# Batch 0's q slots 2 and 3 as one load, permuted on GpSimd; its kv masked by one product; tile 1 turned sooner

## The chip, the core and the metric

The kernel runs on one core of a Trainium2 chip. The metric is the device time of one execution in microseconds (us); five runs of the kernel before gave a median of 294.08.

The core's engines run side by side, each in its own program order: PE (TensorE, matrix multiplications), DVE (VectorE), ACT (ScalarE), POOL (GpSimd) and SP (SyncE, which here only issues transfers). They wait for one another through semaphores. Loads from DRAM are issued here by POOL, since they convert float32 to bfloat16 on the way; stores and transposing transfers are issued by SP. PE's results land in PSUM, where ACT and DVE read them.

## The reference

A linear attention is followed by a two-layer network with a residual:

```python
batch, n_heads, seq, head_dim = (8, 8, 576, 64)     # d_model 512, hidden 2048
kv  = np.einsum('bhsd,bhse->bhde', k, v)            # 64x64 for each head
out = np.einsum('bhsd,bhde->bhse', q, kv)
rms = np.sqrt(np.mean(out * out, axis=-1, keepdims=True) + 1e-06)
x   = out / rms * g_norm                            # then heads side by side: 512 wide
mu, var = mean and variance of x over 512
xn  = (x - mu) / np.sqrt(var + 1e-06) * g_ln
y   = x + np.maximum(xn @ w_ch1, 0.0) @ w_ch2
```

## The kernel before, in words

**Tiles.** The 8 x 576 rows are 36 tiles of 128 rows. A batch gives four tiles, t = 0 to 3, of every fourth row (row 4p + t lies on partition p), and the fifths, the last 64 rows of two neighbouring batches, share a tile. Each tile goes through a chain. `t_out` (PE, L475) multiplies the transposed q (qT) by kv. ACT squares it (`t_sq`, L488), DVE reduces the squares (L497) and multiplies by g_norm (xg, L492), ACT takes the root (L501), DVE the reciprocal (inv, L506) and the product x (L523), then the mean (L535, L539) and xc = (x - mean) * g_ln (L549). xc is transposed: for the first twelve tiles by PE (`t_turn_pe`, L556) and copied to xT by ACT (L563), for later ones by a transposing transfer. The factor 1/std is applied at the end, in `y_out` (L647).

**Main work.** The first layer of tiles 0 to 7 runs tile by tile (`m1_fine`, L606, 16 matmuls of 128 columns for each of four chunks of w1), for later tiles in blocks of four (`m1_block`, L621). ACT evicts with the relu (L613, L628). The second layer is `m2` (L640), four matmuls of 512 columns for each chunk of w2. A chunk, c = 0 to 3, is 512 of the 2048 hidden columns. w1 and w2 are loaded once, chunk by chunk (`load_w`, L343 and L345).

**kv.** `kv_mm` (L452) multiplies k and v of two heads at once, a 128x128 product whose two diagonal blocks of 64x64 are wanted. `kv_out` copies these two blocks into kv_pack, whose other blocks hold zeros. For batch 0 this is done in three parts (heads 0 to 3, 4 and 5, 6 and 7): the upper block by ACT (L465) and the lower by DVE (L467), into a kv_pack that ACT has zeroed (L378).

**q.** For batch 0 each of the slots t = 0 to 3 is a load of its own, straight into the layout that the transposes read (`load_slot`, L262: 64 floats at a time from DRAM). For batch 1 one load brings all four slots (`load_q`, L248) into a buffer qb, and ACT permutes it slot by slot into that layout (`q_permute`, L391). PE transposes a slot (`q_turn_pe`, L411), and ACT or DVE copies the result to qT.

**What sets the order.** The program order on each engine is not the order of the Python code. Every operation is recorded as a step with an engine, an estimated cost, a key (its due place) and the steps that it needs (`add`, L97). `run_plan` (L107) then runs a small simulation: among the steps that can start at the earliest time, the one with the smallest key goes first. On POOL the recorded order is kept as it is, and a step of the main work (`main=True`) keeps its place among the next eight of its kind. At most eight transfers of POOL are under way at a time: an issue waits until the one eight before it has landed. Before the first main step, PE's gaps in the plan are filled with matmuls on a blank tile (`idle_mm`, L961), in numbers taken from the plan.

So a changed load, cost or key can move instructions on all engines. Around the change, POOL's program is: k, v and slot 0 of batch 0 in parts, the identity, slot 1 (L262), then chunks of w1 and slots 2 and 3 in turn, six memsets (L380 to L385), and `load_w_kv1` (L351): w2 chunk 0, k and v of batch 1, w2 chunk 1, q of batch 1 and the rest of w2.

Tile 0 is worked in two halves of heads (`HALVED`, L53). Tiles 0 and 1 have xc and its turn in two halves (`HALF_TURN`, L55). `behind_first` (L667) ties the turn of q's slot 2 behind the turn of tile 0.

Of the kernel before, what the change touches and what calls it, by code (L numbers as in the profile page):

```python
# [14 lines left out]
def kernel(  # L15
# [11 lines left out]
    nc = tc.nc  # L27
# [177 lines left out]
    nc.vector.memset(eps_attn, EPS_ATTN)  # L205
    eps_ln = consts.tile([128, 1], f32, name="eps_ln")
    nc.vector.memset(eps_ln, EPS_LN)
    warm = consts.tile([128, 1], f32, name="warm")
    nc.scalar.activation(warm, eps_ln, func=AF.Sqrt)

# [97 lines left out]
    load = {}  # L308
# [30 lines left out]
    def load_w(c, which):  # L339
        dst, src = ((w1, w1_src), (w2, w2_src))[which - 1]  # L340
        def fn():
            if which == 1:
                nc.gpsimd.dma_start(dst[c], src[:, :, c * 512:(c + 1) * 512])  # L343
            else:
                nc.gpsimd.dma_start(dst[c], src[:, c * 4:(c + 1) * 4, :])  # L345
        pool_load(("w", which, c), (fn, 512 * 512 * 4))
# [2 lines left out]
        make_identity(nc, identity)  # L349

    def load_w_kv1():  # L351
        load_w(0, 2)
        pool_load(("k", 1), load_kv(kb, k, 1), rate6)
        pool_load(("v", 1), load_kv(vb, v, 1), rate6)
        load_w(1, 2)
        pool_load(("q", 1), load_q(1, 0, 4), rate4, [])
        load_w(2, 2)
        load_w(3, 2)
# [6 lines left out]
    pool_load(("v", 0, 6), load_kv(vb, v, 0, 6, 8), rate6)  # L365
    pool_load(("q", 0, 0, 4), load_slot(qp[0], q, 0, 0, 4, 8), rate1)
    ident = pool_do(0.6, identity_fn)
    pool_load(("q", 0, 1), load_slot(qp[0], q, 0, 1), rate1)
    load_w(0, 1)
    pool_load(("q", 0, 2), load_slot(qp[0], q, 0, 2), rate1)  # L370
    load_w(1, 1)
    pool_load(("q", 0, 3), load_slot(qp[0], q, 0, 3), rate1)
    load_w(2, 1)
    load_w(3, 1)


    z0 = add("ACT", 0.5, 0.6, -90, [],
             lambda: nc.scalar.memzero(kv_pack[0].rearrange("p a b -> p (a b)")))  # L378
    z1 = [pool_do(0.5, f) for f in (
        lambda: nc.gpsimd.memset(qp[0][no_fifth(0), 4, :, :], 0.0),  # L380
        lambda: nc.gpsimd.memset(qp[1][no_fifth(1), 4, :, :], 0.0),
# [78 lines left out]
    def kv_out(b, h0, h1, eng, upper):  # L460
        dst, src = kv_pack[b % 3], att[b]["kv", h0]
        p = slice(D, 128) if upper else slice(0, D)
        f = slice(D, 128) if upper else slice(0, D)
        if eng is nc.scalar:
            eng.copy(dst[p, h0:h1, f], src[p, h0:h1, f])  # L465
        else:
            eng.tensor_copy(dst[p, h0:h1, f], src[p, h0:h1, f])  # L467

    def t_out(n, h0=0, h1=H):
        bs, t = TILES[n]  # L470
# [190 lines left out]
    for h0, h1 in PARTS:  # L661
        add_q_turn_pe(0, 0, load["q", 0, 0, h0], -57 + h0 / 4, ("DVE", "ACT")[h0 // 4], h0, h1)
    for t in (1, 2, 3):
        q_turned = add_q_turn_pe(0, t, load["q", 0, t], (-4.5, pos[1] - 3.7, pos[3] - 9)[t - 1],
                                 ("ACT", "ACT", "DVE")[t - 1])
        if t == 2:
            behind_first = q_turned  # L667
    kvs = []

    urgent = []  # L670
    for i, (h0, h1) in enumerate(((0, 4), (4, 6), (6, 8))):
        hps = range(h0 // 2, h1 // 2)
        w = (h1 - h0) / 8
        s = add("PE", 1.36 * w, 1.36 * w + 0.25, -60 + i, load["v", 0, h0] + [k0p[h0 // 4]],
                lambda hps=hps, i=i: kv_mm(0, hps), alloc="kvt")
        ab = [s]
        for u in (0, 1):
            eng, cost = (("DVE", dve_cost), ("ACT", act_cost))[u]
            ab.append(add(eng, *cost(64 * (h1 - h0) // 2), -59 + i, [s, z0],
                          lambda h0=h0, h1=h1, u=u: kv_out(  # L680
                              0, h0 // 2, h1 // 2, (nc.vector, nc.scalar)[u], u == 1)))
        s.frees = ab[-1]
        kvs.append(ab[1:])
        if i == 0:
            kv_first = s
        else:
            urgent.append(s)
        kv_mm_done = s
# [104 lines left out]
    def plan_tile(n):  # L793
# [15 lines left out]
        for h0, h1 in halves:  # L809
            hh = dict(h0=h0, h1=h1)  # L810
            w = (h1 - h0) / H
            q0 = p - 12 if n // 4 in FINE else okey[n]
            d = kvs[len(xs)] + [adone[0]["qT", 0][len(xs)]] if n in HALVED else deps
            o = add("PE", 0.23 * len(bs) * w, 0.23 * len(bs) * w + 0.2, okey[n], d,
                    lambda hh=hh: t_out(n, **hh), alloc="out")
            if n in HALVED:
                urgent.append(o)
            sq = add("ACT", *cost(act_cost, h0, h1), q0 + 4,
                     [o] + [done[n - 3]["red"] if n >= 3 else None], lambda hh=hh: t_sq(n, **hh))
            red = add("DVE", 0.6 * w, 0.6 * w + 0.08, q0 + 5, [sq], lambda hh=hh: t_red(n, **hh))  # L820
            o.frees = xg = add("DVE", *cost(dve_cost, h0, h1), q0 + 5.5, [sq, gn_done],
                               lambda hh=hh: t_xg(n, **hh))
            rms = add("ACT", 0.2, 0.3, q0 + 5.8, [red], lambda hh=hh: t_rms(n, **hh))
            inv = add("DVE", 0.12, 0.2, q0 + 6.5, [rms], lambda hh=hh: t_inv(n, **hh))
            xdeps = [inv, xg]
            if n >= XB:
                xdeps.append(done[n - XB]["store"])
            extra = 0.08 if n < N_SUM else 0
            occ, dur = cost(dve_cost, h0, h1)
            xs.append(add("DVE", occ + extra, dur + extra, q0 + 7, xdeps, lambda hh=hh: t_x(n, **hh)))  # L830
        for b in bs:
            adone[b].setdefault("outs", []).append(o)
        dn["red"] = red
# [4 lines left out]
        for h0, h1 in ((0, 4), (4, 8)) if n in HALF_TURN else halves:  # L838
            ff = dict(f0=h0 * D, f1=h1 * D)
            w = (h1 - h0) / H  # L840
            xc = add("DVE", 0.6 * w + 0.06, 0.6 * w + 0.15, q0 + 8, [mean, load["gl"][0]],
                     lambda ff=ff: t_xc(n, **ff))
            if n < N_PE_TURN:
                tp = add("PE", 0.23 * w, 0.23 * w + 0.22, q0 + 8.2, [xc, ident, m1_before],
                         lambda ff=ff: t_turn_pe(n, **ff), alloc="kvt")
                if n in HALVED:
                    urgent.append(tp)
                tp.frees = add("ACT", *cost(act_cost, h0, h1), q0 + 8.5, [tp],
                               lambda ff=ff: t_turn_out(n, **ff))
# [95 lines left out]
    for i, (kind, a, c) in enumerate(groups):  # L945
# [4 lines left out]
                need_tile(4 * a + j)  # L950
        plan_group(i, kind, a, c)

    for s in late_turns:
        s.deps.append(mains_made[pos[8] - 31])

# [53 lines left out]
```

## Time and profile before

| | |
|---|---|
| median of five runs | 294.08 us (293.97 to 295.35) |
| the profiled execution: time | 294.68 us |
| the profiled execution: span of its instructions | 292.9 us |
| PE busy | 286.6 us (98%) |
| DVE, ACT, POOL busy | 164.3, 143.4, 66.8 us |
| first group of the first layer (L606) starts | 18.32 us |
| loads by POOL (queue 0) | 18.35 MB written |

Times within the profile count from the first instruction. A row of a timeline has the start, the time that the merged instructions span, the engine, the line, the operation, what it writes and reads, shapes, the number of instructions, and in brackets how long the engine idled before and what ended that. PEld is the load of PE's weights. A row of waits names the engine and line that waited, what it waited for, the total, the number and the longest. The chain follows the work that ended last back from the last instruction; "DMA" there is the time from a transfer's issue to its landing, and "issue" is time that the profile puts down to nothing. L and a number is a line of the kernel before.

### The profile page before, as it was taken

How to read it: one execution, taken by the hardware profiler on the slowest of the kernel's cores; microseconds unless marked ns; L12 is line 12 of the kernel's file. 1: busy time of each engine (PE TensorE's matmuls, PEld its weight loads, DVE VectorE, ACT ScalarE, POOL GpSimd, SP SyncE). 2: the span in 40 equal slices, each digit the busy share in tenths (PEclk: the TensorE clock that was granted, in tenths of full speed). 3: DMA queues.
4: the chain of work that ended last, by engine and by line, in shares of the span. 5: the costliest groups of instructions: out<-in, count | busy, mean ns of one | idle time of the engine just before them, and what ended most of it. 6: DMA issues, size and time to landing. Idle time of an engine off the chain costs nothing.

```text
span 292.9 us, 5180 instructions
## 1 busy us (share of the span) xinstructions
PE 286.6 (98%) x2056; PEld 164.5 (56%) x2056; DVE 164.3 (56%) x358; ACT 143.4 (49%) x292; POOL 66.8 (23%) x93
## 2 busy tenths in 40 slices
PE   8899999999999999999999999999999999999995
PEld 6789944977745445444544445444554444444444
DVE  1398038569973997557655775477557755320022
ACT  3279943787846612761276127611761177007400
POOL 8992230105508204504051406000000000000000
PEclk9999999999999999999999999999999999999999
DMA  6999999944999998995999599912201310220012
GB/s 92 176 196 205 204 199 175 253 76 73 173 214 111 163 128 196 139 166 132 174 114 167 95 172 132 191 54 91 56 18 54 92 54 18 57 83 25 0 74 72
DMA packets 108716, 35.60 MB, mean 122 GB/s; under 512 B 87187, under 2 KB 104467, under 8 KB 108692
## 3 DMA queue, kind: packets, MB, share of 16 engines
q0 software_dynamic: 72624, 18.35, 66.0%
q1 hardware_dynamic: 35828, 16.79, 25.6%
q8 instruction: 16, 0.26, 0.4%
q10 hardware_dynamic: 240, 0.13, 0.2%
q14 instruction: 8, 0.07, 0.1%
HBM read 36.70 MB, written 9.44 MB: 158 GB/s over the span
## 4 chain that ended last, share of the span: by engine, by line
PE 85%; DMA 9%; POOL 4%; issue 0%; ACT 0%; DVE 0%; POOLq 0%
PE mm_ps L640 41%; PE mm_ps L621 33%; DMA qb<-in_q_dram 7%; PE mm_ps L606 5%; PE out_ps L475 3%; DMA kb<-in_k_dram 2%; PE kv_ps L452 2%; POOL w L343 1%; PE xT_ps L556 1%; POOL kb L241 1%; POOL vb L241 0%; POOL w L345 0%; POOL qp L262 0%; PE qT_ps L411 0%; ACT qp L391 0%
## 5 line engine op out<-in xcount | busy, mean ns | idle before, releaser
L640 PE MATMUL mm_ps<-w,m 128*128 128x512 bf16 (+2 forms) x608 | 129.8, 368 | 0.0
L621 PE MATMUL mm_ps<-xT,w 128*128 128x512 bf16 x448 | 100.6, 379 | 0.0
L628 ACT ACTIVATE m<-mm_ps 128x512 bf16<-128x512 f32 x112 | 66.9, 598 | 51.1 <-PE mm_ps L621 50.3
L640 PEld LDWEIGHTS <-m 128*128 128x128 bf16 x608 | 57.1, 98 | 60.4
L621 PEld LDWEIGHTS <-w 128*128 128x128 bf16 x448 | 43.1, 98 | 48.9
L497 DVE TENSOR_REDUCE ss<-sq 128x8 f32<-128x512 f32 (+1 forms) x37 | 24.7, 669 | 47.7 <-ACT sq L488 47.7
L647 DVE SCALAR_TENSOR_TENSOR x<-mm_ps,rstd,x 128x512 f32<-128x512 f32 (+2 forms) x38 | 27.3, 720 | 42.1 <-PE mm_ps L640 42.1
L488 ACT ACTIVATE sq<-out_ps 128x512 f32<-128x512 f32 (+1 forms) x37 | 21.5, 584 | 39.5 <-PE out_ps L475 39.4
L606 PE MATMUL mm_ps<-xT,w 128*128 128x128 bf16 x512 | 30.9, 219 | 0.3
L606 PEld LDWEIGHTS <-w 128*128 128x128 bf16 x512 | 29.4, 98 | 1.5 <-issue 0.7
L549 DVE SCALAR_TENSOR_TENSOR xc<-x,mv,gl 128x512 bf16<-128x512 f32 (+1 forms) x38 | 27.2, 723 | 1.1
L492 DVE TENSOR_TENSOR xg<-out_ps,gn 128x512 f32<-128x512 f32 (+1 forms) x37 | 24.7, 668 | 0.2
L730 POOL COPY mark<-xT 128x1 bf16<-128x1 bf16 x15 | 7.4, 491 | 57.1 <-DMA xT<-xc 53.1
L613 ACT ACTIVATE m<-mm_ps 128x512 bf16<-128x512 f32 x32 | 18.7, 597 | 3.3 <-PE mm_ps L606 2.9
L527 DVE TENSOR_TENSOR x<-xg,inv 128x512 f32<-128x512 f32 x24 | 16.6, 692 | 0.8
L501 ACT ACTIVATE rms<-ss,eps_attn 128x8 f32<-128x8 f32 (+1 forms) x37 | 11.1, 299 | 12.1 <-DVE ss L497 11.9
L543 DVE BATCH_NORM_STATS2 stats<-x 128x6 f32<-128x512 f32 x24 | 16.6, 690 | 0.5
L475 PEld LDWEIGHTS <-qT 128*128 128x128 bf16 x160 | 11.7, 100 | 6.9 <-ACT qT L391 0.7
L475 PE MATMUL out_ps<-kv_pack,qT 128*128 128x128 bf16 x160 | 15.0, 224 | 0.5 <-ACT qT L391 0.5
L452 PEld LDWEIGHTS <-kp 128*128 128x128 bf16 (+1 forms) x168 | 11.3, 105 | 2.6 <-issue 0.9
L467 DVE CAST kv_pack<-kv_ps 64x256 bf16<-64x256 f32 (+2 forms) x17 | 6.6, 390 | 10.7 <-PE kv_ps L452 5.7
L452 PE MATMUL kv_ps<-vb,kp 128*128 128x128 bf16 (+1 forms) x144 | 11.9, 234 | 0.6 <-DMA vb<-in_v_dram 0.5
(63 smaller groups left out, 183.8 us busy)
## 6 DMA issues: line engine op xcount, KB each, us to landing
out_dram<-x SPq DMA_DIRECT2D x30, 256.0 KB, 2.9
w<-in_moe_w_ch_dram POOLq DMA_DIRECT2D x8, 512.0 KB, 12.1
vb<-in_v_dram POOLq DMA_DIRECT2D x6, 512.0 KB, 11.3
kp<-in_k_dram POOLq DMA_DIRECT2D x5, 512.0 KB, 9.0
qp<-in_q_dram POOLq DMA_DIRECT2D x5, 512.0 KB, 10.5
out_dram<-x SPq DMA_DIRECT2D x10, 128.0 KB, 3.1
qb<-in_q_dram POOLq DMA_DIRECT2D x2, 512.0 KB, 18.0
qp<-in_q_dram POOLq DMA_DIRECT2D x10, 64.0 KB, 9.0
```

What stands on the lines that cost most here:

```text
L452: nc.tensor.matmul(ps[:, hp, :], lhsT=kp[b % 2][p, t, 2 * hp:2 * hp + 2, :].rearrange("p h d -> p (h d)"), rhs=(v5[b % 2][:, 2 * hp:2 * hp ...
L475: nc.tensor.matmul(o3[:, hp, :], lhsT=att[b]["qT"][:, 4 * t + hp, :], rhs=kv_pack[b % 3][:, hp, :], start=(i == 0), stop=(i == len(bs) - 1))
L488: nc.scalar.activation(sq[:, h0:h1, :], st[n]["ps", h0][:, h0:h1, :], func=AF.Square)
L492: nc.vector.tensor_mul(xg[:, h0:h1, :], st[n]["ps", h0][:, h0:h1, :], gn.to_broadcast([128, h1 - h0, D]))
L497: nc.vector.tensor_reduce(ss[:, h0:h1, :], st[n]["sq"][:, h0:h1, :], axis=AX.X, op=ALU.add)
L549: nc.vector.scalar_tensor_tensor(xc[:, f0:f1], in0=st[n]["x"][:, f0:f1], scalar=blk[m]["mv"][:, i, 0:1], in1=gl[:, f0:f1], op0=ALU.subtrac ...
L606: nc.tensor.matmul(ps[:, d, :], lhsT=w1[c][:, kk, d * 128:(d + 1) * 128], rhs=blk[m]["xT"][:, kk, i * 128:(i + 1) * 128], start=(kk == 0), ...
L613: nc.scalar.activation(st[n]["m1"][:, c, :, :], st[n]["m1ps", c], func=AF.Relu)
L621: nc.tensor.matmul(ps, lhsT=w1[c][:, kk, d * 128:(d + 1) * 128], rhs=blk[m]["xT"][:, kk, :], start=(kk == 0), stop=(kk == nKm - 1))
L628: nc.scalar.activation(blk[m]["m1", c][:, d, :], blk[m]["m1ps", g], func=AF.Relu)
L640: nc.tensor.matmul(st[n]["m2ps", f0], lhsT=m1_piece(n, c, d), rhs=w2[c][:, d, f0:f1], start=(c == 0 and d == 0), stop=(c == 3 and d == 3))
L647: nc.vector.scalar_tensor_tensor(x[:, f0:f1], in0=st[n]["m2ps", f0], scalar=blk[m]["rstd"][:, i, :], in1=x[:, f0:f1], op0=ALU.mult, op1=AL ...
```

## The change

- Slots 2 and 3 of batch 0's q become one load into qb, issued right behind slot 1 and so ahead of all of w1. POOL permutes them, slot by slot, into the layout for the transposes (`q0_slot`).
- The four chunks of w1 follow one another; w2 chunk 0 and k and v of batch 1 are issued before POOL's permutes and memsets rather than behind the memsets.
- kv of batch 0: instead of two copies for each part, one DVE product of the whole PSUM part with a mask of ones on the two diagonal blocks (`diag`, filled by DVE at the start). ACT's zeroing of kv_pack goes.
- Keys: the first half of x gets 4.8 in place of 7, and the turn of tile 1 gets -3.5, a fixed place ahead of the main work. The turn of q's slot 3 is tied behind the second main step.

As the plan comes out, PE has the turn of tile 1 (all four transposes) between the out of tile 2 and the second chunk of tile 0; it stood behind that chunk, in two halves around the turn of slot 3. Slot 3's turn comes behind chunk 2 of tile 0. For batch 1, PE has the turns of slots 0 and 1 together and, four matmuls of L640 later, both outs; before, each turn was followed by its own out, with four and eight matmuls of L640 in between. DVE's order is the same up to xc of tile 1 but for the products in place of copies.

```diff
+    diag = consts.tile([128, 1, 128], f32, name="diag")
+    nc.vector.memset(diag, 0.0)
+    for p in (slice(0, D), slice(D, 128)):
+        nc.vector.memset(diag[p, :, p], 1.0)
...
     def load_w_kv1():
-        load_w(0, 2)
-        pool_load(("k", 1), load_kv(kb, k, 1), rate6)
-        pool_load(("v", 1), load_kv(vb, v, 1), rate6)
         load_w(1, 2)
         pool_load(("q", 1), load_q(1, 0, 4), rate4, [])
...
     ident = pool_do(0.6, identity_fn)
-    pool_load(("q", 0, 1), load_slot(qp[0], q, 0, 1), rate1)
-    load_w(0, 1)
-    pool_load(("q", 0, 2), load_slot(qp[0], q, 0, 2), rate1)
-    load_w(1, 1)
-    pool_load(("q", 0, 3), load_slot(qp[0], q, 0, 3), rate1)
-    load_w(2, 1)
-    load_w(3, 1)
-    z0 = add("ACT", 0.5, 0.6, -90, [],
-             lambda: nc.scalar.memzero(kv_pack[0].rearrange("p a b -> p (a b)")))
+    pool_load(("q", 0, 1), load_slot(qp[0], q, 0, 1), 240.0)
+    pool_load(("q", 0, 2), load_q(0, 2, 4), rate4)
+    for c in range(QUADS):
+        load_w(c, 1)
+    load_w(0, 2)
+    pool_load(("k", 1), load_kv(kb, k, 1), rate6)
+    pool_load(("v", 1), load_kv(vb, v, 1), rate6)
+
+    q0_slot = {t: pool_do(0.7, lambda t=t: q_permute(nc.gpsimd, 0, t, t + 1), load["q", 0, 2])
+               for t in (2, 3)}
...
+    def kv_out_masked(b, h0, h1):
+        nc.vector.tensor_mul(kv_pack[b % 3][:, h0:h1, :], att[b]["kv", h0][:, h0:h1, :],
+                             diag.to_broadcast([128, h1 - h0, 128]))
...
     for t in (1, 2, 3):
-        q_turned = add_q_turn_pe(0, t, load["q", 0, t], (-4.5, pos[1] - 3.7, pos[3] - 9)[t - 1],
+        q_turned = add_q_turn_pe(0, t, [q0_slot[t]] if t > 1 else load["q", 0, t], (-4.5, pos[1] - 3.7, pos[3] - 9)[t - 1],
                                  ("ACT", "ACT", "DVE")[t - 1])
         if t == 2:
             behind_first = q_turned
+        elif t == 3:
+            behind_second = q_turned
...
-        ab = [s]
-        for u in (0, 1):
-            eng, cost = (("DVE", dve_cost), ("ACT", act_cost))[u]
-            ab.append(add(eng, *cost(64 * (h1 - h0) // 2), -59 + i, [s, z0],
-                          lambda h0=h0, h1=h1, u=u: kv_out(
-                              0, h0 // 2, h1 // 2, (nc.vector, nc.scalar)[u], u == 1)))
-        s.frees = ab[-1]
-        kvs.append(ab[1:])
+        s.frees = add("DVE", *dve_cost(64 * (h1 - h0)), -59 + i, [s],
+                      lambda h0=h0, h1=h1: kv_out_masked(0, h0 // 2, h1 // 2))
+        kvs.append([s.frees])
...
-            xs.append(add("DVE", occ + extra, dur + extra, q0 + 7, xdeps, lambda hh=hh: t_x(n, **hh)))
+            xs.append(add("DVE", occ + extra, dur + extra, q0 + (4.8 if h1 < H else 7), xdeps, lambda hh=hh: t_x(n, **hh)))
...
-                tp = add("PE", 0.23 * w, 0.23 * w + 0.22, q0 + 8.2, [xc, ident, m1_before],
+                tp = add("PE", 0.23 * w, 0.23 * w + 0.22, -3.5 if n == 1 else q0 + 8.2, [xc, ident, m1_before],
                          lambda ff=ff: t_turn_pe(n, **ff), alloc="kvt")
...
+    behind_second.deps.append(mains_made[1])
     for s in late_turns:
         s.deps.append(mains_made[pos[8] - 31])
```

More of the change, by code (lines that the diff above doesn't have):

```diff
@@ L462, in kv_out @@
         p = slice(D, 128) if upper else slice(0, D)
[L463 to L467, printed above, removed]
+        eng.tensor_copy(dst[p, h0:h1, p], src[p, h0:h1, p])
+    def kv_out_masked(b, h0, h1):
+        nc.vector.tensor_mul(kv_pack[b % 3][:, h0:h1, :], att[b]["kv", h0][:, h0:h1, :],
+                             diag.to_broadcast([128, h1 - h0, 128]))
     def t_out(n, h0=0, h1=H):
```

## The prediction

> **What bounds the kernel now.** I read the page's busy table first (PE is busy 98% of the span), then the chain that ended last, then PE's waits, and after that the timelines of PE, DVE, ACT and POOL up to 45 us. PE's timeline is what matters:
>
> ```profile
> 15.87 1.88 PE L961 MATMUL idle_ps<-blank 128*128 128x128 bf16 x18
> ...
> 18.32 1.22 PE L606 MATMUL mm_ps<-xT,w 128*128 128x128 bf16 x16
> 19.37 0.39 PE L475 MATMUL out_ps<-kv_pack,qT 128*128 128x128 bf16 x4
> 19.59 1.06 PE L606 MATMUL mm_ps<-xT,w 128*128 128x128 bf16 x16
> 20.48 0.28 PE L556 MATMUL xT_ps<-identity,xc 128*128 128x128 bf16 x2
> 20.60 0.39 PE L411 MATMUL qT_ps<-identity,qp 128*128 128x128 bf16 x4
> 20.87 0.28 PE L556 MATMUL xT_ps<-identity,xc 128*128 128x128 bf16 x2
> 21.22 1.34 PE L606 MATMUL mm_ps<-xT,w 128*128 128x128 bf16 x16
> ```
>
> From the first expert group at 18.32 on, PE hardly stops. A group of 16 takes 0.89 (16 at 55.5 ns, as in the rows of many groups), a turn or an out of four 0.22. By these the rows lose 0.16 in the first group (second half of xT), then about 0.56 around tile 1's turn: 20.48 to 22.39 is 1.91 for 0.22 + 0.22 + 0.89. Together 0.72. The last loss is at 40.11:
>
> ```profile
> PE qT_ps L411 <- ACT qp L391: 0.5, 1, 0.5
> ```
>
> Starts of matmuls put it at 0.62. The chain tells why: batch 1's q lands at 39.41.
>
> ```profile
> 19.70 19.71 DMA qb<-in_q_dram
> 39.41 0.02 issue
> 39.44 0.63 ACT qp L391
> ```
>
> So after 18.32 there are 1.34 us to win, and nothing else but a sooner 18.32. From 40.11 on the chain is PE without a gap; any shift there is the shift of the end.
>
> Tile 0's and tile 1's own work runs on DVE without a pause:
>
> ```profile
> 15.80 0.42 DVE L523 CUSTOM_DVE_ANT_1 x<-xg,inv 128x256 f32<-128x256 f32 x1
> ...
> 16.52 0.88 DVE L549 SCALAR_TENSOR_TENSOR xc<-x,mv,gl 128x256 bf16<-128x256 f32 x2
> ...
> 19.93 0.88 DVE L549 SCALAR_TENSOR_TENSOR xc<-x,mv,gl 128x256 bf16<-128x256 f32 x2
> ```
>
> Tile 1's xc ends at 20.81, and its second turn starts at 20.87: the turn goes when DVE is done, not when PE is free.
>
> **The change part by part.**
>
> *kv of batch 0.* Three pairs of copies (ACT 0.26, 0.21, 0.21, each followed by DVE 0.28, 0.22, 0.22, one after the other) become three DVE products of 256, 128, 128 columns. The row of xg, 128x256 from PSUM, is 0.41; 128 columns fewer at 0.96 per ns make 0.28. The last pair ran 13.10 to 13.56; the product runs 13.10 to 13.38, so the first reduce (13.48) starts 0.16 sooner, and all of DVE's chain with it: its order up to tile 1's xc is the same. Tile 0 gains nothing: the second half's out waits for ACT's qT copy, which waits for PE, and the 18 idle matmuls, the same number in both, hold PE until 17.58 while xc of tile 0 ends at 17.40 (then 17.24). First group: 18.32 as before, 0. The zeroing on ACT (0.40 at 2.15) and the three memsets of the mask on DVE lie in idle time (DVE idles 3.7 before 4.82): 0.
>
> *Loads.* Landings by issue plus time to landing: slot 1 of q at 13.4, w1 chunk 0 at 15.9, slot 2 at 16.8, chunk 1 at 19.3, slot 3 at 20.2, chunk 2 at 22.7, chunk 3 at 25.2; a chunk takes 2.5. The two slots cost 0.84 + 0.91 = 1.75 in the queue. As one load they cost between 1.35 (half of batch 1's q, 2.7 for twice the bytes in pieces twice as long) and 1.75; I take 1.40, nearer the load of its own form. Chunk 0 then lands at 17.3 (needed 18.3, hidden), chunk 1 at 19.75 instead of 19.3, chunk 2 at 22.3, and all behind it 0.35 sooner (bounds 0 and 0.4): batch 1's q at 39.05. The queue is never empty up to there, so w2's chunk 1 and batch 1's q, issued behind the permutes at about 19.5 and 20.3 instead of 18.95 and 19.70, lose nothing: they waited 17.8 and 19.7 to land.
> By the Trainium skill (DMA: Bandwidth & Descriptors, section Specifications) transfers run at line rate from 512 B on, which the joined load's reads reach and a slot's do not. By that it would cost half a chunk, 1.25, batch 1's q would land at 38.9 and the +0.43 below would be +0.28; no row here has this form.
>
> *Permutes on GpSimd.* POOL's issues take 0.90 (slot or q form), 0.77 (w), 0.8 (k, v). From 6.99: slot 1, joined q, chunk 0 until 9.55, chunk 1 at 9.99 (it waits for a landing at 9.71) to 11.15, then chunks 2, 3, w2's chunk 0, k and v of batch 1 until 15.0. The joined q has landed at 14.8. So two permutes start at 15.0, and six memsets (13.57 to 16.7 before) come behind. One permute: no such row; a POOL memset of 128x512 took 0.52 without reading, a select of 128x128 0.49, which scales to 1.4. ACT's same copy took 0.61; I take 0.7, ends 0.52 and 1.4. Slots 2 and 3 are in place by 16.4, before PE wants them: 0 there. But they run beside x (15.64) and xc (16.36) of tile 0. What such neighbours cost, the start of the trace shows:
>
> ```profile
> 6.17 0.72 DVE L393 COPY kp<-kb 96x1536 bf16<-96x1536 bf16 x1 [1.12 <-DMA kb<-in_k_dram]
> 6.20 0.27 POOL masks.py:197 MEMSET identity<- 128x128 bf16 x1
> 6.55 0.49 POOL masks.py:199 TENSOR_SCALAR_AFFINE_SELECT identity<-identity 128x128 bf16<-128x128 bf16 x1
> ...
> 10.29 0.54 DVE L393 COPY kp<-kb 96x1536 bf16<-96x1536 bf16 x1
> ...
> 15.74 0.52 POOL L384 MEMSET kv_pack<- 128x512 bf16 x1
> ```
>
> The same DVE copy took 0.18 more beside POOL's work; x took 0.42 beside a memset and no longer than elsewhere. If x or xc wait while a permute reads: x loses 0.06 (slot 2 ends at 15.7), slot 3 gets in behind x, 16.1 to 16.8, and xc loses 0.4. I call this c and take 0.45; ends 0 (no row shows x waiting) and 1.8 (two permutes of 1.4).
> The Trainium skill speaks against the change here (SBUF — State Buffer, section Who interferes with whom): a DVE instruction with two SBUF inputs contends with a GpSimd instruction that reads SBUF, not with one that only writes, and whoever is second is blocked fully. x beside the memsets agrees with its second half; the first half no row here shows on DVE's side. By it c is 0.45 with a permute of 0.7 and the time 295.0; without it c is 0 and the time 294.5.
>
> *Tile 1's turn.* It now stands on PE right behind out of tile 2, ahead of chunk 1 for tile 0. PE is there at 18.32 + 0.16 + 0.89 + 0.22 = 19.59. xc of tile 1 ends at 20.81 − 0.16 + c, its turn at 20.82 + c. Wait 1.01 + c. It covers the 0.45 by which chunk 1 is late, and the 0.56 of before goes. Net +0.45 + c for PE's arrival at batch 1's q: 39.49 before its wait of 0.62, now 39.94 + c. Slot 3's turn behind chunk 2 and the later evictions on ACT keep 0.3 us or more of room.
>
> *Batch 1's q.* PE now has both turns together, four matmuls, then both outs; before, 1.73 of w2 work lay between, and the second out started at 43.38. Its qT copy on ACT stands behind all four permutes:
>
> ```profile
> 39.44 2.17 ACT L391 COPY qp<-qb 128x512 bf16<-128x512 bf16 x4 [2.67 <-DMA qb<-in_q_dram]
> 41.85 0.59 ACT L391 COPY qT<-qT_ps 128x512 bf16<-128x512 bf16 x1 [0.24 <-PE qT_ps L411]
> ```
>
> From a landing at 39.05: permutes until 41.25, a std (0.2), the copy until 42.05, out at 42.1. The 1.73 is still to do: 42.1 + 1.73 − 43.38 = +0.43, whatever PE did before. PE alone gives 39.94 + c − 40.11 = −0.17 + c. The end moves by the larger: +0.43 at c = 0.45.
>
> **Sum.** The profiled execution took 294.68 (span 292.9, 1.8 around it), 0.60 above the median 294.08 of five runs (293.97, 293.99, 294.08, 294.68, 295.35). Against itself: 295.1. The median lacks 0.60; the one loss of that size which a landing sets is the 0.62, so I take it that the median runs do not have it. Then PE's arrival counts in full: 294.08 + 0.45 + 0.45 = 295.0. If the 0.60 lies in both kernels: 294.5.
>
> **Rivals.**
> - *The permutes don't disturb DVE* (c = 0). For: x beside memsets is not stretched, POOL's spans are rough. Against: the copy at 6.17. Then +0.43 to +0.45, 294.5.
> - *They disturb it more*, permutes of 1.0 to 1.4: c 1.0 to 1.8, 295.5 to 296.3. For: the select's 0.49 for a quarter of the columns. Against: it ran beside that copy itself.
> - *The joined load saves nothing* (1.75): the floor becomes +0.78, chunk 1 lands at 20.1, still inside the turn's wait. 295.5 against the profiled execution, 294.9 to 295.2 by the median.
> - *Faster: tile 1's turn finds xc ready.* If xc ends by 19.59, PE has no wait there, and with q's 0.35 sooner none at 40: of 1.34 only 0.16 stays, 294.08 − 1.18 = 292.9. It decides at 1.06 us sooner on DVE's tile 1 chain; for it speaks only that the runs differ by 1.4 us and one was profiled; the chain gains 0.16 by the rows.
>
> **Chances.** Forecast 0.42 (294.6 to 295.5 by c and the landing), no disturbance 0.17, more 0.17, load 0.09, faster 0.15. Faster and slower begin 0.3% off, which is about what a measurement of this kernel can tell from no change: 293.2 and 294.96. The forecast's range is cut there, 0.24 slower and 0.18 same; load 0.06 and 0.03. Faster 0.15, same 0.38, slower 0.47. From 293.6 to 296.1, 0.15 is left out below and some 0.04 above.
>
> **What would show it.** PE waits 1 to 1.5 us for DVE's xc at about 19.6; first group at 18.3 to 18.5; POOL copies of 128x512 at 15, 0.5 to 1.4 each; x or xc of tile 0 later than 15.64 and 16.36 by c; chunk 1 landed near 19.75, batch 1's q near 39.05; out behind ACT's qT copy at about 42. I am wrong if the turn of tile 1 does not wait, or if a new gap of PE appears past 45 us.

## The result, and the profile after

| | before | changed |
|---|---|---|
| median | 294.11 us (48 runs) | 294.89 us (26 runs) |
| ratio of the runs | | 1.0023, 95% interval 1.0015 to 1.0031 |
| the profiled execution: time, span | 294.68, 292.9 us | 294.40, 292.6 us |

The changed kernel is slower by 0.7 us (0.4 to 0.9), a small loss that is clear of zero and still inside the 0.3% that the prediction called no change, the upper end of the interval just outside it. Its profiled execution is nevertheless 0.28 us faster than the one shown of before. A second profile of each kernel (below) shows which of these four executions is the odd one, and the comparison of the profiles rests on it.

PE's timeline of the changed kernel, ahead of the first group and at batch 1 (start, span, engine, line and operation, in brackets the idle time before and what ended it):

```profile
16.45 0.68 PE L559 MATMUL xT_ps<-identity,xc 128*128 128x128 bf16 x4 [1.45 <-DVE xc L552]
16.96 0.39 PE L414 MATMUL qT_ps<-identity,qp 128*128 128x128 bf16 x4
17.19 1.34 PE L609 MATMUL mm_ps<-xT,w 128*128 128x128 bf16 x16
18.36 0.39 PE L478 MATMUL out_ps<-kv_pack,qT 128*128 128x128 bf16 x4
19.59 0.68 PE L559 MATMUL xT_ps<-identity,xc 128*128 128x128 bf16 x4 [0.84 <-DVE xc L552]
...
36.86 2.75 PE L643 MATMUL mm_ps<-w,m 128*128 128x512 bf16 x12
39.45 0.61 PE L414 MATMUL qT_ps<-identity,qp 128*128 128x128 bf16 x8
39.90 1.03 PE L643 MATMUL mm_ps<-w,m 128*128 128x512 bf16 x4
40.76 0.89 PE L478 MATMUL out_ps<-kv_pack,qT 128*128 128x128 bf16 x8
```

The first group of the first layer starts at 17.19, not at 18.32. Tile 1's turn, now ahead of tile 0's chunk 1, waits for DVE's xc: by the starts of the matmuls 1.00 us before it and 0.27 between its halves. At batch 1 both turns stand in one piece and both outs in one piece. Eight matmuls of an out take 0.61 where nothing interrupts them; here 0.89, because the second four wait 0.27 for ACT's copy of qT. (Such a gap between matmuls is called a bubble below.) The chain that ended last of the same kernel shows what that copy stands behind (start, length, piece):

```profile
19.24 19.09 DMA qb<-in_q_dram
38.33 0.02 issue
38.35 2.17 ACT qp L394 x4
40.53 0.20 ACT std L594
40.73 0.48 ACT qT L394
41.20 0.05 issue
41.25 0.40 PE out_ps L478 x4
```

Batch 1's q lands at 38.33, all four permutes run, a root, the copy, and then the second out goes, 2.92 us after the landing. From there to the end PE has no gap worth naming. That a landing can pace all this is seen in the page's row of the DMA engines' busy tenths (40 slices of 7.3 us):

```profile
DMA  6999999955999997992999299912201310120012
```

From 7 us to 58 us they have no slice under nine tenths: the loads of the start queue up, and each lands when those ahead of it are through.

POOL's permutes and DVE's x, from the timeline of all engines:

```profile
12.90 0.42 DVE L526 CUSTOM_DVE_ANT_1 x<-xg,inv 128x256 f32<-128x256 f32 x1
...
14.07 1.25 POOL L396 COPY qp<-qb 128x512 bf16<-128x512 bf16 x2
...
14.24 1.37 DVE L526 CUSTOM_DVE_ANT_1 x<-xg,inv 128x256 f32<-128x256 f32 x1
...
15.90 0.88 DVE L552 SCALAR_TENSOR_TENSOR xc<-x,mv,gl 128x256 bf16<-128x256 f32 x2
```

The first half of x took 0.42; the second half, started while POOL copied, took 1.37 and ended after both copies had. The two xc behind it, beside POOL's memsets, took 0.88 as before.

### The profile page after: what moved, and what is told of

Same layout as the page of the kernel before. It is cut to its first block, busy times and chain, and to the rows that moved or that the text cites. A ratio compares the mean times of both kernels' runs of the same rounds, so it can differ in the third digit from the quotient of the medians.

```text
span 292.6 us, 5181 instructions
## 1 busy us (share of the span) xinstructions
PE 284.3 (97%) x2056; PEld 161.7 (55%) x2056; DVE 166.4 (57%) x361; ACT 142.7 (49%) x288; POOL 66.1 (23%) x94
## 4 chain that ended last, share of the span: by engine, by line
PE 85%; DMA 7%; POOL 6%; ACT 1%; issue 0%; DVE 0%; POOLq 0%
PE mm_ps L643 41%; PE mm_ps L624 33%; DMA qb<-in_q_dram 7%; PE mm_ps L609 5%; PE out_ps L478 3%; PE kv_ps L455 2%; POOL w L348 1%; POOL vb L246 1%; POOL kb L246 1%; POOL qp L267 1%; ACT qp L394 1%; PE xT_ps L559 1%; POOL w L350 0%; POOL qp L396 0%; POOL qb L253 0%
## 5 line engine op out<-in xcount | busy, mean ns | idle before, releaser
L730 POOL COPY mark<-xT 128x1 bf16<-128x1 bf16 x15 | 6.7, 445 | 57.6 <-DMA xT<-xc 53.8
L466 DVE CAST kv_pack<-kv_ps 64x256 bf16<-64x256 f32 x14 | 5.9, 422 | 12.1 <-PE kv_ps L455 12.0
L455 PEld LDWEIGHTS <-kp 128*128 128x128 bf16 (+1 forms) x168 | 10.7, 102 | 2.1 <-issue 0.3
L455 PE MATMUL kv_ps<-vb,kp 128*128 128x128 bf16 (+1 forms) x144 | 11.3, 227 | 0.4 <-DMA vb<-in_v_dram 0.3
```

The source lines that it names most:

```text
L455: nc.tensor.matmul(ps[:, hp, :], lhsT=kp[b % 2][p, t, 2 * hp:2 * hp + 2, :].rearrange("p h d -> p (h d)"), rhs=(v5[b % 2][:, 2 * hp:2 * hp ...
```

## The experiments

In all experiments but the two repeats the order that the planner had given the kernel was written out as a list and only the named steps were moved in it; otherwise one changed key reorders the whole program. Where only the order moved, the cut below names the steps that moved; the list itself is not shown. Each was timed beside the kernel before on the same chip; the ratios are to that. Line numbers are those of the kernel in question.

### Each kernel once more

> The changed kernel once more, for a second profiled execution. If its sooner first m1 group (17.19 against 18.32 us) came from loads that happened to land 0.7 to 1.0 us sooner in that one execution, this profile has the first group anywhere between 17 and 18.5 us, and tile 0's x takes about 0.95 us more than its half at 0.42 again, because the two GpSimd permutes stand beside it by order. If the change itself brings the start forward, the first group stands at 17.2 us again. The ratio is 1.0023 again, within 0.001.

> The kernel before once more, for a second profiled execution. The first one was 294.68 us against a median of 294.0 to 294.1, and had a stall of 0.62 us at batch 1's q. Theory: that stall was chance; here q lands by 38.9 us, PE does not stop at batch 1, the span is 292.2 to 292.5 us, and the first m1 group stands at 17.9 to 18.4 us again because the order of VectorE and ScalarE ahead of it is the same. Rival (the stall is always there): a bubble of 0.5 us or more at batch 1's q and a span of 292.9. The ratio is 1.000 within 0.0008.

Measured: the changed kernel 294.47 us (11 runs, ratio 1.0015, 1.0007 to 1.0024), the kernel before 293.96 (12 runs, ratio 0.9998, 0.9989 to 1.0006). These two profiled executions took 294.47 and 294.05, each within 0.1 us of the median of its runs, so they are the pair to compare. PE's timeline of the kernel before, second profile:

```profile
13.93 1.17 PE L961 MATMUL idle_ps<-blank 128*128 128x128 bf16 x18
15.74 0.68 PE L556 MATMUL xT_ps<-identity,xc 128*128 128x128 bf16 x4 [0.65 <-DVE xc L549]
16.26 0.39 PE L411 MATMUL qT_ps<-identity,qp 128*128 128x128 bf16 x4
16.49 1.33 PE L606 MATMUL mm_ps<-xT,w 128*128 128x128 bf16 x16
17.66 0.39 PE L475 MATMUL out_ps<-kv_pack,qT 128*128 128x128 bf16 x4
19.06 1.07 PE L606 MATMUL mm_ps<-xT,w 128*128 128x128 bf16 x16 [1.01 <-DMA w<-in_moe_w_ch_dram]
...
39.51 0.40 PE L411 MATMUL qT_ps<-identity,qp 128*128 128x128 bf16 x4 [0.45 <-ACT qp L391]
```

The eighteen idle matmuls take 1.17 here against 1.88 in the first profile, and the first group stands at 16.49 against 18.32: the first profile was the odd one, for in the four later profiles of kernels in the order of before the group stands at 16.28 to 16.86. (The Trainium skill, TensorE: Matmul & The Clock Gate, Part 1, says that the array warms up in a window which runs freely, so that the same kernel has more or fewer slow matmuls from run to run. The 1.88 and the 1.17 agree with that; the granted clock does not show it, it reads 1.00 in both from 12 us on.) What did not change is the stall at batch 1. Starts of matmuls put it at 0.62 us in both. PE came 0.6 us sooner to it, and batch 1's q landed 0.6 us sooner as well, at 38.81 against 39.41. My theory that the stall was chance fell, and with it an assumption of the prediction.

The chain of this execution from that landing on:

```profile
19.30 19.52 DMA qb<-in_q_dram
38.81 0.02 issue
38.84 0.63 ACT qp L391
39.46 0.05 issue
39.51 0.40 PE qT_ps L411 x4
```

PE's first turn stands at the landing + 0.70, in both profiles of before. So the kernel before, too, is paced by q's landing and not by PE's early waits.

Changed kernel, second profile: first group at 17.45, x's second half 1.22, tile 1's turn waiting 1.00 and 0.27, q landed at 38.37, a bubble of 0.24 ahead of the second out. Its start is not chance: against 16.49 it is 0.7 to 1.0 us later in both profiles.

### The permutes on ScalarE

```diff
-    q0_slot = {t: pool_do(0.7, lambda t=t: q_permute(nc.gpsimd, 0, t, t + 1), load["q", 0, 2])
+    q0_slot = {t: pool_do(0.7, lambda t=t: q_permute(nc.scalar, 0, t, t + 1), load["q", 0, 2])
                for t in (2, 3)}
```

In ScalarE's order the two stand behind the square of tile 1.

> The two permutes of slots 2 and 3 on ScalarE, which is idle from 14.6 to 16.8 us, instead of GpSimd; every other instruction in the changed kernel's order. Theory (the path through tile 0): x falls from 1.37 to 0.42 us, tile 0's turn stands 0.5 to 0.95 us sooner, and the end moves by what the wait for batch 1's q leaves of it. Rival 1 (x is held by something other than the GpSimd copies): x stays at about 1.3 us and the time at 1.002. Rival 2 (batch 1's q sets the end): x falls to 0.42 us, the PE bubble ahead of batch 1's second out grows from 0.27 to 0.8 us or more, and the time stays within 0.1 us of the changed kernel's.

Measured: 294.85 us (12 runs), ratio 1.0027 (1.0014 to 1.004). DVE and ACT, from the timeline of this kernel:

```profile
14.76 0.43 DVE L526 CUSTOM_DVE_ANT_1 x<-xg,inv 128x256 f32<-128x256 f32 x1
...
15.00 1.13 ACT L394 COPY qp<-qb 128x512 bf16<-128x512 bf16 x2
```

and PE's timeline, further on:

```profile
22.00 1.07 PE L609 MATMUL mm_ps<-xT,w 128*128 128x128 bf16 x16 [0.36 <-DMA w<-in_moe_w_ch_dram]
...
39.44 0.61 PE L414 MATMUL qT_ps<-identity,qp 128*128 128x128 bf16 x8
```

x is back at 0.43: the POOL copies are what held it. (The Trainium skill, SBUF — State Buffer, section Who interferes with whom, says that a DVE instruction with two SBUF inputs contends with a GpSimd instruction that reads SBUF, and not with one that only writes it. The held x beside the copies, the free x here and the free xc beside the memsets agree.) The turn of tile 0 came sooner and the time did not. But the gain was not lost where Rival 2 put it: the bubble at batch 1 stayed at 0.24. It was lost at 22.00, where PE now waits 0.53 for w1 chunk 2 (landed at 21.95), and PE reaches batch 1 at 39.44 as before.

### Tile 1's turn behind chunk 1 again

```diff
 PE's order: out of tile 2
+m1 of tile 0, chunk 1
 turn of tile 1
-m1 of tile 0, chunk 1
 m1 of tile 1, chunk 0
```

> One PE group moved: tile 0's m1 chunk 1 ahead of tile 1's turn again, every other instruction in the changed kernel's order. Theory (the early waits are on the path): the 1.0 and 0.27 us that PE waits for tile 1's xc shrink to under 0.4 in all, w1 chunk 1 (landing at 19.5) costs up to 0.5 us itself, and the time falls by 0.4 to 0.9 us. Rival (batch 1's q sets the end): the early waits shrink just so, the bubble ahead of batch 1's second out grows by as much, and the time stays within 0.15 us of the changed kernel's.

Measured: 294.74 us (12 runs), ratio 1.0023 (1.0012 to 1.0034).

```profile
19.49 1.07 PE L609 MATMUL mm_ps<-xT,w 128*128 128x128 bf16 x16 [0.72 <-DMA w<-in_moe_w_ch_dram]
20.39 0.39 PE L559 MATMUL xT_ps<-identity,xc 128*128 128x128 bf16 x4
21.13 2.11 PE L609 MATMUL mm_ps<-xT,w 128*128 128x128 bf16 x32 [0.35 <-ACT xT L566]
```

Neither expectation held in full. The waits did not shrink, they changed their owner: 0.88 for w1 chunk 1 (landed 19.45), 0.51 for ACT's copy of xT. The time stayed, and PE was at batch 1 at 39.48. The wait of tile 1's turn, which the prediction charged to the change, costs nothing in this order that the landings of chunks 1 and 2 would not have cost.

### Batch 1's second qT copy on VectorE

```diff
-                    add_q_turn_pe(1, t, [qperm, z1[1]], key + 1, ("DVE", "ACT")[t % 2])
+                    add_q_turn_pe(1, t, [qperm, z1[1]], key + 1, "DVE")
```

> Batch 1's second qT copy on VectorE instead of ScalarE, where it stands behind four permutes and a square root; every other instruction in the changed kernel's order. Theory (the second out sets a floor at the landing of batch 1's q plus 1.48 us of this chain): the copy ends 0.3 to 0.5 us sooner, the PE bubble of 0.27 us ahead of the second out goes, and the time falls by 0.25 to 0.45 us. Rival (the early PE waits set the end): the copy ends sooner, and the time stays within 0.15 us.

Measured: 294.97 us (8 runs), ratio 1.0034 (1.0022 to 1.0046): the second out waits no more (its eight matmuls take 0.61), and the time is no better. The chain of this kernel's profiled execution says what took over:

```profile
10.38 12.09 DMA w<-in_moe_w_ch_dram
22.46 0.05 issue
22.51 1.07 PE mm_ps L609 x16
```

Not q's load but w1 chunk 2, landed at 22.46, and from there PE without a gap to the end. In the changed order PE has only three groups to do before it needs chunk 2, where the kernel before has four. So there are two limits, and this table of the profiled executions shows them (landings and starts in us, from the traces; the stall at batch 1 is included in PE's first turn):

| kernel | w1 chunk 1 | w1 chunk 2 | batch 1's q | PE's first turn there | last matmul ends | end − q's landing | first turn − chunk 2 |
|---|---|---|---|---|---|---|---|
| before | 19.28 | 22.71 | 39.41 | 40.11 | 289.41 | 250.00 | |
| before, again | 19.01 | 22.06 | 38.81 | 39.51 | 288.81 | 250.00 | |
| before, masked kv alone | 19.57 | 22.57 | 39.02 | 39.72 | 289.02 | 250.00 | |
| changed | 19.54 | 22.06 | 38.33 | 39.45 | 289.11 | 250.78 | 17.39 |
| changed, again | 19.60 | 22.12 | 38.37 | 39.52 | 289.21 | 250.84 | 17.40 |
| permutes on ScalarE | 19.41 | 21.95 | 38.29 | 39.44 | 289.02 | 250.73 | 17.49 |
| turn behind chunk 1 | 19.45 | 21.97 | 38.48 | 39.48 | 289.21 | 250.73 | 17.51 |
| slots not joined | 20.16 | 22.66 | 39.07 | 40.11 | 289.80 | 250.73 | 17.45 |
| both copies on VectorE | 19.94 | 22.46 | 38.51 | 39.86 | 289.25 | (not the limit) | 17.40 |

Three executions of the order of before end exactly 250.00 after q's landing, five of the changed order 250.73 to 250.84 after it. And in the changed order PE is in no execution at batch 1 sooner than 17.39 us after w1 chunk 2 lands. In the five where q's chain was the limit, the second out waited 0.24 to 0.38 for it; the other limit lies no further off than that. So lifting q's chain alone could give 0.24 to 0.27 in the changed kernel, and in the execution shown w1 chunk 2 landed 0.34 to 0.40 later than in that kernel's two profiles, which takes up as much. Whether all eight runs had so late a landing is not known, and the other limit was not lifted alone.

### The masked kv alone, on the kernel before

```diff
             ab.append(add(eng, *cost(64 * (h1 - h0) // 2), -59 + i, [s, z0],
-                          lambda h0=h0, h1=h1, u=u: kv_out(
-                              0, h0 // 2, h1 // 2, (nc.vector, nc.scalar)[u], u == 1)))
+                          lambda h0=h0, h1=h1, u=u: None if u else kv_out_masked(
+                              0, h0 // 2, h1 // 2)))
```

The mask is filled as in the changed kernel, and ScalarE's zeroing goes.

> The kernel before with batch 0's kv masked by one VectorE product instead of a ScalarE and a VectorE copy each; no load, turn or queue is moved. The prediction's step gave this 0.16 us on VectorE and nothing at the first m1 group. Theory from the five profiles of changed kernels (x's first half at 13.3 to 13.4 us against 14.46, with the k half landing alike): the pair of copies ran one after the other and held the second k permute behind it; x's first half stands 0.9 to 1.1 us sooner here too and the first m1 group at 17.2 to 17.8 us. What comes of it: 0.3 to 0.6 us faster if PE's work from there to batch 1 is unbroken, within 0.15 us if the landing of w1 chunk 1 (19.3) or 2 (22.7) takes it back. Rival (the prediction's step): x's first half 0.16 us sooner, the first group at 18.3, the time the same.

Measured: 294.29 us (12 runs), ratio 1.0011 (1.0002 to 1.0021). DVE's timeline here with the last product, and behind it the second profile of the kernel before with the last copy in its place:

```profile
11.83 0.29 DVE L475 TENSOR_TENSOR kv_pack<-kv_ps,diag 128x128 bf16<-128x128 f32 x1 [0.47 <-PE kv_ps L457]
...
13.02 0.42 DVE L532 CUSTOM_DVE_ANT_1 x<-xg,inv 128x256 f32<-128x256 f32 x1
```

```profile
12.02 0.21 DVE L467 CAST kv_pack<-kv_ps 64x64 bf16<-64x64 f32 x1 [0.71 <-ACT kv_pack L465]
...
13.14 0.42 DVE L523 CUSTOM_DVE_ANT_1 x<-xg,inv 128x256 f32<-128x256 f32 x1
```

x's first half is 0.12 us sooner, although PE's last kv matmuls started 0.05 later (11.29 against 11.24): from them to x it is 0.17 less. My theory, made from the odd first profile, fell; the prediction's 0.16 on DVE is right. Nothing comes of it: the first group is at 16.37, and then PE idles 1.68 for w1 chunk 1, which landed at 19.57 in this execution.

### The slots not joined

```diff
-    pool_load(("q", 0, 2), load_q(0, 2, 4), rate4)
+    pool_load(("q", 0, 2), (lambda: [load_slot(qp[0], q, 0, t)[0]() for t in (2, 3)],
+                            2 * 128 * 512 * 4), rate4)
...
-    q0_slot = {t: pool_do(0.7, lambda t=t: q_permute(nc.gpsimd, 0, t, t + 1), load["q", 0, 2])
+    q0_slot = {t: pool_do(0.7, lambda t=t: None, load["q", 0, 2])
```

> The changed kernel with slots 2 and 3 loaded as two slots straight into their places instead of one joined load, at the same place in the queue ahead of the weights, and without the GpSimd permutes; every other instruction in the changed kernel's order. By the prediction's terms the joined load saves 0.35 us of queue, and the permutes cost tile 0's x 0.45 us (0.80 to 0.95 in the traces). Theory (landings set the pace): w1 chunk 2 and batch 1's q land 0.25 to 0.5 us later, x takes 0.42 us, and the time is 0.2 to 0.5 us above the changed kernel's. Rival (the permutes' hold on x is what costs): 0.3 us or more faster than the changed kernel.

Measured: 295.04 us (9 runs), ratio 1.0034 (1.0021 to 1.0048). x takes 0.43; w1 chunk 2 lands at 22.66 and q at 39.07, 0.5 to 0.6 and 0.7 later than in the changed kernel's two profiles; the profiled execution ends 0.6 to 0.7 us later than those (last matmul). The rival, by which x's hold is what costs, is excluded: the time did not fall. The theory is not shown by the time, whose interval overlaps that of the changed kernel's first runs (1.0015 to 1.0031), and only in small part by the queue: the two slots took 0.95 + 0.65 = 1.60 there, against 1.49 and 1.42 for the joined load, and the rest of the 0.7 came in with the weights behind, w1 chunk 0 above all, which landed 4.04 us behind the slots in this one execution. In the second profile of before the two slots, at their old places, took 0.83 + 0.55 = 1.38 (slot 2 landed at 15.81 behind chunk 0 at 14.98, slot 3 at 19.56 behind chunk 1 at 19.01). So the runs leave open whether joining them saves time in the queue.

### Batch 1's q ahead of w2 chunk 1, on the kernel before

```diff
     def load_w_kv1():
-        load_w(1, 2)
         pool_load(("q", 1), load_q(1, 0, 4), rate4, [])
+        load_w(1, 2)
         load_w(2, 2)
```

> The kernel before with batch 1's q loaded ahead of w2 chunk 1 instead of behind it; nothing else moved. Batch 1's q lands 2.4 to 2.7 us sooner (36.7 to 37.0), w2 chunk 1 as much as 0.3 us after 39.2. Theory (in most executions of before PE does not wait for this q): the time stays within 0.15 us, or loses up to 0.3 us where w2 chunk 1 is now late. Rival (before waits for it in most executions): 0.4 to 0.6 us faster.

Measured: 295.98 us (6 runs), ratio 1.0061 (1.0042 to 1.008). Both expectations missed. q landed at 36.21, the stall went, and PE was past batch 1 0.8 us sooner (second out at 42.01 against 42.78). Then PE stopped for batch 2:

```profile
59.69 0.38 PE L452 MATMUL kv_ps<-vb,kp 128*128 128x128 bf16 x4 [0.40 <-DMA vb<-in_v_dram]
60.59 0.22 PE L452 MATMUL kv_ps<-v,kp 128*128 128x128 bf16 x1 [0.51 <-DMA v<-in_v_dram]
```

Batch 2's v landed at 59.65 against 52.13. With q, ACT's four permutes came sooner, and with them SyncE's transposing transfer of slots 2 and 3, which they release. Its rows here, and in the kernel before's second profile:

```profile
38.43 1.34 SPq L433 DMA_TRANSPOSE qT<-qp  x1
```

```profile
41.04 1.34 SPq L433 DMA_TRANSPOSE qT<-qp  x1
```

One more kernel moved four things of the changed kernel at once: its permutes of slots 2 and 3 to ScalarE, batch 1's q ahead of w2 chunk 1, both qT copies of batch 1 to VectorE, and tile 1's chunk 1 ahead of tile 0's chunk 2, so that PE has four groups ahead of w1 chunk 2. Lifting both limits was expected to give 293.2 to 293.7. Measured: 295.46 us (7 runs), ratio 1.0045 (1.0021 to 1.007): a miss. q landed at 36.53, PE did not wait for w1 chunk 2 (landed at 22.49), and the two outs went in one piece; but PE was at batch 1 only at 40.12, 0.6 later than in the changed kernel. w1 chunk 1 landed at 19.96 in this execution, 0.36 later than in the second profile of that kernel, and there were new waits, one of them on PE's timeline:

```profile
24.50 0.40 PE L478 MATMUL out_ps<-kv_pack,qT 128*128 128x128 bf16 x4 [0.52 <-DVE qT L396]
```

Behind batch 1, k and v of batch 2 landed later here too (50.63 and 53.77, against 49.11 and 52.70 in the second profile of the changed kernel). With so much moved at once, this run doesn't say what lifting the two limits is worth.

### Holding that transfer back

Two attempts to hold the transfer back by moving ACT's permutes of slots 2 and 3 behind the copy of qT, one on each kernel (the kernel before with batch 1's q ahead of w2 chunk 1, as above; the changed kernel with q at its place):

```diff
 ACT's order at batch 1: permutes of slots 0, 1
-permutes of slots 2, 3
 copy of qT (slot 1), square of tile 4
+permutes of slots 2, 3
```

On the changed kernel slot 3's turn and tile 1's chunk 1 were also moved ahead of tile 0's chunk 2.

> The changed kernel with both of its limits at batch 1 moved at once, by order alone: (1) slot 3's turn and tile 1's m1 chunk 1 ahead of tile 0's chunk 2, so that PE has four groups ahead of w1 chunk 2's landing; (2) on ScalarE the permutes of batch 1's slots 2 and 3 behind the qT copy of slot 1 and tile 4's square, so that the second out no longer waits through them. Theory (w1 chunk 2's landing + 17.4 us and q's landing + 1.48 us are two limits within 0.3 us of each other, and taking one away, as in the runs before, shows the other): no wait for w1 chunk 2, no bubble at the second out, and 0.3 to 0.6 us faster than the changed kernel, 293.9 to 294.2, a ratio of 1.000 within 0.001. Rival (the cost is later than batch 1): the bubbles go and the time stays at 294.5 to 294.9.

> The kernel before with batch 1's q ahead of w2 chunk 1 as in the run that was 2 us slower, and the permutes of its slots 2 and 3 on ScalarE behind the second qT copy and the square that follows, so that SyncE's turn of slots 2 and 3 (a DMA) starts at about 42.5 us instead of 38.43 (before: 41.04). Theory (in that run the turn's DMA ran into the last weight loads and held batch 2's v back to 59.65 us from 52.13): batch 2's v lands by 53.5 us, the bubbles from 58.9 to 71 us go, the 0.62 us stall at batch 1 stays away, and the time is 293.2 to 293.6, a ratio of 0.997 to 0.9985: faster than both kernels. Rival (q's place in the queue itself delays batch 2): v lands at 56 us or later and the time stays above 294.5.

Measured: 305.86 and 305.77 us, ratios 1.0399 (1.0376 to 1.0421) and 1.0389 (1.0369 to 1.0408). In both I had overlooked that the load of batch 2's q into the same buffer then stood ahead of the two permutes; they waited for it, and permuted batch 2's q in place of batch 1's. ACT in the second one:

```profile
53.59 1.14 ACT L391 COPY qp<-qb 128x512 bf16<-128x512 bf16 x2 [11.75 <-DMA qb<-in_q_dram]
```

The times are those of this wait and decide nothing on the two limits; that both, lifted together, give the changed kernel back its 0.4 us is left open. One row of the first is still of use, since it comes before the wait: with only two permutes ahead of the copy the eight matmuls of the two outs took 0.61, so the second out no longer waits.

The repaired form on the kernel before moves one permute and puts the load of batch 2's q behind it:

```diff
 POOL's order: k and v of batch 1
-w2 chunk 1
 q of batch 1
+w2 chunk 1
 ACT's order at batch 1: permutes of slots 0, 1, 2
-permute of slot 3
 copy of qT (slot 1)
+permute of slot 3
 square of tile 4
```

SP's transfer of slots 2 and 3 and POOL's load of batch 2's q stand behind that permute.

> The kernel before with batch 1's q ahead of w2 chunk 1, and of its four ScalarE permutes only the one of slot 3 moved, behind the second qT copy; SyncE's turn of slots 2 and 3, which needs it, and the load of batch 2's q, which overwrites what it reads, both stand behind it. Theory (q's landing + 0.70 us is what holds PE for 0.62 us in the kernel before, and the 2 us lost when q alone was moved came from SyncE's turn starting at 38.43 us): q lands at 36.0 to 36.9, no stall at batch 1, SyncE's turn starts at 41.2 to 41.8 us, batch 2's v lands by 53.5 us, and the time is 293.2 to 293.7, a ratio of 0.997 to 0.999, faster than both kernels. Rival 1 (q's place in the queue itself delays batch 2): v at 56 us or later and 295 or more. Rival 2 (tile 4's square, 0.5 us later behind the permute, becomes the wait): the stall goes, a bubble of 0.3 to 0.6 us stands at tile 4's turn, and the time is 293.8 to 294.2.

Measured: 293.67 us (11 runs), ratio 0.9992 (0.9982 to 1.0001). PE's timeline, and behind it SP's:

```profile
19.21 1.07 PE L606 MATMUL mm_ps<-xT,w 128*128 128x128 bf16 x16 [1.43 <-DMA w<-in_moe_w_ch_dram]
...
36.45 2.76 PE L640 MATMUL mm_ps<-w,m 128*128 128x512 bf16 x12
39.05 0.39 PE L411 MATMUL qT_ps<-identity,qp 128*128 128x128 bf16 x4
```

```profile
41.91 1.33 SPq L433 DMA_TRANSPOSE qT<-qp  x1
```

The stall is gone, the transfer starts at 41.91, batch 2's v lands at 52.62, and no new gap appears. Its median is the lowest of all, 0.3 us below the kernel before on the same chip (293.98) and 0.8 to 1.2 below the changed kernel; but its interval against before just reaches 1, so a gain over before is likely and not shown. The chain now goes through w1 chunk 1 (landed at 19.17): PE's first turn at batch 1 is 19.88 us after that landing, as it would be without the stall in the second profile of before (39.51 − 0.62 − 19.01). That is before's other limit, and it is why 0.62 could not be had in full. That SP's transfer was what delayed batch 2 in the earlier run is supported by this pair of runs; what passes between the transfers was not measured by itself.

## Why the prediction was right or wrong

The forecast was 295.0 us, +0.9; the ratio of 1.0023 makes it +0.7, the second set of runs +0.5. No change within 0.3% had been given 0.38, slower 0.47.

- **The floor at batch 1 (the chain from q's landing to the second out): right, and it decides in the changed kernel's two profiles.** The prediction's shift was 0.78 less the sooner landing of q. The table has 250.73 to 250.84 against 250.00, which is 0.73 to 0.84.
- **q's landing: sooner about as forecast, but not by the step that the prediction took.** Forecast 0.35 sooner; 0.44 in the pair of typical executions (38.81 to 38.37). For that pair the floor gives 0.84 − 0.44 = +0.40, and last matmuls end 0.39 apart, executions 0.42. The step was that the joined load saves 0.35 in the queue and brings all behind it forward by as much. The joined load took 1.49 and 1.42 for the 1.40 taken, but the two slots took 1.38 in the second profile of before, not the first one's 1.75. In the pair nothing was gained up to batch 1's v, which landed at 32.98 before and at 33.01 after; the 0.44 came in behind it, with w2 chunk 1 (in the queue 3.15 before, 2.83 after) and q itself (2.68, 2.53). Why these two took less is open, and that the size came out is luck. (By the sentence from the Trainium skill, DMA: Bandwidth & Descriptors, Specifications, the estimate for the joined load was 1.25; the measurement is nearer the row-based price.)
- **The median's missing stall: wrong.** The step "I take it that the median runs do not have it" failed: an execution at the median has the same 0.62. The right sum is the median + 0.43 = 294.5, the variant that the prediction gave to "the 0.60 lies in both kernels". 295.0 came nearer to the 26 runs (294.89) than 294.5 did, but that is luck, for the reason for adding PE's arrival in full was wrong; the later 11 runs (294.47) lie at 294.5.
- **The first group at 18.32 for both: wrong.** It was the odd start of one execution. Typical is 16.49 before and 17.2 to 17.45 after; the cover that I named, eighteen slow idle matmuls until 17.58, is not there in other executions.
- **c: mechanism right, size off.** x was held by the POOL copies, 0.95 and 0.80 instead of 0.45; I had slot 3's permute strike xc, but one x was held through both permutes, which came at 14.07 and 14.36 instead of 15.0. A permute took 0.70, as taken; its upper end of 1.4 does not follow from the row that it was drawn from, since 0.49 for a quarter of the columns would give 1.96. On the time c has no effect: taken away, w1 chunk 2's landing gives the same.
- **Tile 1's turn: the wait is there (1.27; forecast 1.01 + c), its price does not show.** Put back behind chunk 1, PE waits for chunk 1 instead. The prediction's net of +0.45 + c on PE's arrival (0.9 at c = 0.45) is 0.63 against before's 38.89 without its stall, and it is set by a limit which the prediction did not name: three groups instead of four ahead of w1 chunk 2, so arrival no sooner than its landing + 17.4. (DVE's chain, which the prediction read as without a pause, had one of 0.18 at 18.77, for ACT's root.)
- **The masked product: right,** 0.17 for 0.16 on DVE, no gain in the time.
- **The rivals.** Without disturbance of DVE the time was to be 294.5; the run without it gave 294.85, so c had no price that shows. "The joined load saves nothing" is not excluded: 1.38 and 1.60 for two slots lie on both sides of 1.42 and 1.49 for the joined load. What it made of the time, no sooner q and +0.78 for the floor, did not come: q landed at 38.29 to 38.51 in the five profiles with the joined load that the table shows, at 38.81 to 39.41 in the three of the order of before. The faster rival's condition, xc of tile 1 ready, was not met in either profile of the changed kernel.

What stays open: the first 26 runs of the changed kernel had a median of 294.89, the later 11 of 294.47. In the changed order w1 chunk 2's landing counts, in the order of before it has slack, and that landing moves by 0.5 us (21.95 to 22.46) between the table's profiles with the joined load; this fits, but only the profiled executions show landings. Open, too, are why batch 1's q lands sooner in the changed kernel, and what the kernel would gain with both limits lifted.

## What to carry to other kernels

Where a saturated load queue paces the start, write each stage's start as the landing of what it waits for plus a chain, and compare the chains: here 250.00 and 250.8 after one landing explained eight executions when the early waits of PE, 1.3 us of them, explained nothing. Take a second profile before naming a loss: what both have (the stall of 0.62) is the structure, what one has (the first group at 18.32) is chance. And a transfer that comes sooner brings forward all that it releases; hold that back, and its buffer's next load with it, before moving it.

## What the runs showed that I had not expected

- One DVE product of 128x256 with two SBUF inputs, 0.42 by itself, was held to 1.22 and 1.37 through two POOL copies of 0.70 back to back; it did not get in between them.
- Two loads of 1 MB, w1 chunks 0 and 1, land 5.05 to 6.10 us after the joined q in the five profiles that the table shows of that load order (13.87 to 19.54, 14.19 to 19.60, 14.36 to 19.41, 13.75 to 19.45, 13.84 to 19.94), though chunks 2 and 3 behind them take 2.5 each. The excess moves from run to run, and every later landing with it.
- A transposing transfer by SyncE started at 38.43 instead of 41.04 among POOL's loads was followed by landings of batch 2's k and v 2.7 and 7.5 us later (50.97 for 48.24, 59.65 for 52.13).
